# Packing the token-mixing product of a spectral and MLP block to eleven matmuls, with the shift by tokens made in SBUF

## The chip, the core and the metric

The kernel runs on one core of a Trainium2 chip. A core has five engines that run side by side, each with its own queue of instructions, worked off in order: TensorE (matmuls, "PE" in the profile; "PEld" is its loading of the stationary operand), VectorE ("DVE"), ScalarE ("ACT"), GpSimd ("POOL") and SyncE ("SP"), which here issues all DMA transfers. Sixteen DMA engines move the data. Engines wait for one another by semaphores. Matmuls write to PSUM (banks of 128 x 512 float32), the other tiles live in SBUF (128 partitions).

The metric is the device time of one execution in microseconds, as the median of several runs.

## The reference

x has 2048 tokens of 448 channels. It is normalized once (`xn`), and then two branches are added to it: a spectral filter (2-D FFT, product with a complex weight, inverse FFT) and an MLP block with a shift between tokens.

```python
def _A_ref(x, w_r, w_i):
    X = rfft2(x) * (w_r + 1j * w_i)
    return irfft2(X, s=(S, D))

def _B_ref(x, w1, w2, w3, w4):
    h = _gelu(_layernorm(x) @ w1)              # D x D
    c = D // 4                                 # 112 channels
    # four groups of channels, shifted by +1, -1, +2, -2 tokens, zeros come in
    hs = concatenate([g0, g1, g2, g3]) @ w2    # D x D
    x1 = x + hs
    return x1 + _gelu(_layernorm(x1) @ w3) @ w4   # 448 -> 1792 -> 448

xn = _layernorm(x)
out = x + _A_ref(xn, w_r, w_i) + _B_ref(xn, w1, w2, w3, w4)
```

The change touches the first half of `_B_ref`: the product with w1, the gelu, the shift and the product with w2.

## The kernel before

**Tiles.** Token 16a + b lies on partition a of block b: 16 blocks of 128 tokens. A shift by one or two tokens therefore mostly means another block on the same partition; only where the block number wraps (from 15 to 0 or from 0 to 15) the partition moves by one. Blocks are worked in four groups of four, `GRP = [[14, 15, 0, 1], [2, 3, 4, 5], [6, 7, 8, 9], [10, 11, 12, 13]]`. `load_x` loads two blocks at a time.

**Precision.** All large products are made of float16 halves: an operand is split in a high part and a low part (`hi`, `lo`), and a product takes the passes hi x hi, hi x lo and lo x hi (`PASS`), summed in PSUM. ScalarE makes the high part, VectorE (or GpSimd) the low part as a difference. Weights are scaled by a power of two first; `powers` finds it from a sum of squares (`squares`, on ScalarE), a small matmul with a tile of ones and a few steps on VectorE.

**The first half of the MLP block, in stages.**
- `norm1(g, apply)` normalizes a group: statistics on VectorE, then the blocks by the engines in `apply`; `refine` and `scales`, on GpSimd, make a finer scale (`gsc`) and the factor `cs` used later.
- `T1(g)` transposes a group on TensorE (16 transposes) and splits the result into `xT` (`transpose_split`: the high part on ScalarE, the low part on VectorE). The last group goes through `turn`, with DMA transposes.
- `w1_in` multiplies: 11 products of 448 columns for each block, four blocks in a group. For the first group all four blocks go along together, one quarter `t` of the channels after another.
- `w1_unit(g, i)` finishes a block: gelu on ScalarE, high part on ScalarE, low part on VectorE, both into a staging buffer `hs` with each 112-channel group padded to 128; then SP issues one DMA transpose of 8 pieces of 128 x 128 into `h`.
- `w2_tile(b)` multiplies with w2. The shift is made here, by reading for each of the four channel groups another block of `h`, at an offset of one column where the partition moves: four groups, three passes, so 12 products with 112 rows each. VectorE adds the result to xb(b).
- `ln2` is the second layer norm, ending with a DMA transpose for each block into `x2all`; `mlp` runs w3, gelu and w4 for eight pairs of blocks G.

**Order.** Each engine's order is made by a scheduler, which places instructions by priorities and its own estimate of times when the program is built; `behind(...)` holds an instruction back until named others have been issued. After that the order is fixed, so an instruction that waits holds everything behind it on its engine. `warm_up` puts 28 products on zeros at the start of TensorE's queue.

The spectral branch (from `do_fold` on) and the rest of the MLP follow and are not changed but for names of blocks.

Of the kernel before, what the change touches and what calls it, by code (L numbers as in the profile page):

```python
# [25 lines left out]
SHIFT = [1, -1, 2, -2]  # L26
WARM = 28
# [9 lines left out]
HS = 3  # L37
# [31 lines left out]
def constants():  # L69
# [20 lines left out]
    for c in range(NC):  # L90
        for j8, (k1, t) in enumerate(slots(c)):
            for j, (kr, s, base) in enumerate(rows(c)):
                if base != k1:
                    continue
                phi = tau * np.outer(np.arange(NB), kr + 128 * np.arange(16)) / S
# [28 lines left out]
def body(tc, nc, x, wf, w1, w2, w3, w4, c_g, c_n, c_small, out):  # L124
# [81 lines left out]
    SY.dma_start(w2s[:112], w2.rearrange("(k p) n -> p k n", p=112))  # L206
# [14 lines left out]
    x2mem = pw.tile([128, 9 * F], F16, name="x2mem")  # L221
    x2all = x2mem[:, 0:8 * F].rearrange("p (j t n) -> p j t n", j=4, t=7)
    w4raw = x2mem.bitcast(F32)[:, F:].rearrange("p (f n) -> p f n", f=14)
    w4v = w4.rearrange("(f p) n -> p f n", p=128)
    W4F = (0, 4, 8, 11, 14)

    def load_w4(i):
        SY.dma_start(w4raw[:, W4F[i]:W4F[i + 1]], w4v[:, W4F[i]:W4F[i + 1]])
# [164 lines left out]
    w2p = pr.tile([112, 2, 4, D], F16, name="w2p")  # L393
# [3 lines left out]

    def h_alloc(g):
        t = {0: 0, 1: 1, 2: 2, 3: 1}[g]
        hT[g] = pr.tile([128, 8, 512 if g else 592], F16, tag=f"h{t}", name=f"h{g}")  # L400
        if g == 0:
            P.memset(hT[g][:, :, 0:576].rearrange("p t (b a) -> p t b a", b=4)[:, :, :, 0:16], 0.0)
            P.memset(hT[g][:, :, 576:592], 0.0)

    def h_at(g, i):
        return 128 * i if g else 144 * i + 16
# [9 lines left out]

    hs_buf = [p1.tile([128, 2, 4, 128], F16, name=f"hs{i}") for i in range(HS)]
    for t in hs_buf:
        P.memset(t.rearrange("p i k n -> p (i k) n")[:, :, 112:], 0.0)

    for o in (0, 1024):
        hs_buf.append(x2mem[:, o:o + 1024].rearrange("p (i k n) -> p i k n", i=2, k=4))
        P.memset(hs_buf[-1].rearrange("p i k n -> p (i k) n")[:, :, 112:], 0.0)

    def w1_unit(g, i, pm=None):
        if pm is None:
            pm = bank(("tr" if g == 1 else "mm", "acc")[i // 2], f"pw1_{g}{i}")
            w1_in(g, [(i, pm)], range(4))
        c = CS[GRP[g][i]]
        pm = pm[:, :D]  # L430
        pv_ = pm.rearrange("p (k n) -> p k n", k=4)
        h = hs_buf[c % (HS if g == 3 else HS + 2)]
        A.activation(out=pm, in_=pm, func=AF.Gelu_apprx_tanh, scale=gsc[:, c:c + 1])
        u = A.activation(out=h[:, 0, :, 0:112], in_=pv_, func=AF.Copy, scale=h1)
        v = V.scalar_tensor_tensor(out=h[:, 1, :, 0:112], in0=pv_, scalar=h1, in1=h[:, 0, :, 0:112],
                                   op0=ALU.mult, op1=ALU.subtract)
        o = h_at(g, i)
        d = SY.dma_start_transpose(out=hT[g][:, :, o:o + 128], in_=h.rearrange("p i k n -> p (i k n)"))
        after[g, i] = u.ins, v.ins
        after["h", g, i] = (d.ins,)  # L440

    def w2_tile(b):
        pm = bank("sp", f"pw2_{b}")
        n = 0
        for k in (2, 0, 1, 3):
            src, o = b - SHIFT[k], 1
            if src < 0:
                src, o = src + NB, 0
            elif src >= NB:
                src, o = src - NB, 2  # L450
            g, i = WHERE[src]
            o += h_at(g, i) - 1
            for hi, wi in ((0, 0), (0, 1), (1, 0)):
                T.matmul(pm[:, :D], hT[g][:112, 4 * hi + k, o:o + 128], w2p[:, wi, k], start=n == 0, stop=n == 11)  # L454
                n += 1
        V.scalar_tensor_tensor(out=xb(b), in0=xb(b), scalar=cs[:, CS[b]:CS[b] + 1], in1=pm[:, :D],
                               op0=ALU.mult, op1=ALU.add)

    def ln2(bs, engines):
# [22 lines left out]
        for i in range(n):  # L482
            b, h, x_ = b0 + i, y[i // 2][:, i % 2], o[i // 2][:, i % 2]
            k = r[:, i:i + 1]
            u = A.activation(out=h[:, 0:D], in_=x_, func=AF.Copy, scale=k)
            V.scalar_tensor_tensor(out=h[:, 448:512], in0=x_[:, 384:448], scalar=k, in1=h[:, 384:448],
                                   op0=ALU.mult, op1=ALU.subtract)
            v = V.scalar_tensor_tensor(out=h[:, 512:896], in0=x_[:, 0:384], scalar=k, in1=h[:, 0:384],
                                       op0=ALU.mult, op1=ALU.subtract)
            d = SY.dma_start_transpose(out=x2all[:, b // 4][:, :, 128 * (b % 4):128 * (b % 4) + 128], in_=h)  # L490
            after[f"b{b0}"] = u.ins, v.ins, d.ins

    def unscale(p, part):
        t = part.rearrange("p (b n) -> p b n", b=2)
        SY.dma_start(t, xv[:, 2 * p:2 * p + 2])
        return lambda: V.scalar_tensor_tensor(out=xt[p], in0=xt[p], scalar=p12, in1=t, op0=ALU.mult, op1=ALU.add)

    def finish(b):
        t = xb(b)
        if b < 2:  # L500
            t = row()[:, :D]
            SY.dma_start(t, xv[:, b])
            V.scalar_tensor_tensor(out=t, in0=xb(b), scalar=p12, in1=t, op0=ALU.mult, op1=ALU.add)
        SY.dma_start(ov[:, b], t)
# [6 lines left out]
    def do_fold(b0):  # L511
        X = pfd.tile([128, 2, D + 1], F32, tag="xf", bufs=3, name=f"xf{b0}")
        after["X", b0] = (SY.dma_start(X[:, :, 0:D], xv[:, b0:b0 + 2]).ins,)
# [181 lines left out]
    def front(G, fp, tag):  # L695
        tok = slice(256 * (G % 2), 256 * (G % 2) + 256)
        pm = bank(tag, f"pw3_{G}{fp}")
        for ff in range(2):
            f = 2 * fp + ff
            mlp_in(pm[:, 256 * ff:256 * ff + 256], w3p, slice(128 * f, 128 * f + 128), x2all[:, G // 2], tok)  # L700
# [66 lines left out]
    def back(G, fp):  # L767
# [10 lines left out]
        for i in range(2):  # L778
# [12 lines left out]
            if end:  # L791
                with prio(EVAC):
                    for r, to in parts:
                        V.scalar_tensor_tensor(out=xb(b)[:, r], in0=to, scalar=p34[:, min(G, 1):min(G, 1) + 1],  # L794
                                               in1=xb(b)[:, r], op0=ALU.mult, op1=ALU.add)
                        if G > 4:
                            SY.dma_start(ov[:, b, r], xb(b)[:, r])
# [51 lines left out]
    def w4_split(f):  # L849
        split_w(w4p[0][:, 0, f:f + 2], w4p[0][:, 1, f:f + 2], w4raw[:, f:f + 2], s4)  # L850
# [7 lines left out]
    h_alloc(0)  # L858
# [8 lines left out]
    for t in range(4):  # L867
        w1_in(0, list(enumerate(first)), [t])
    n1[0][0]()
    with behind("w1", 1):  # L870
        n1.append(norm1(1, [P, V, A, V]))
    with behind("w1", 3):
        squares(m2[:112], flat(w2s[:112]))
# [20 lines left out]
    h_alloc(1)  # L894
# [10 lines left out]
    h_alloc(2)  # L905
# [17 lines left out]
    for b in range(4, 8):  # L923
        w2_tile(b)
        with behind(*PIN[b - 4]):
            w3_split(2 * b - 8)
            w3_split(2 * b - 7)
            for i in (2 * b - 10, 2 * b - 9):
                if i >= 0:
                    squares(m4[:, i:i + 1], flat(w4raw[:, 2 * i:2 * i + 2]), junk4)  # L930
    squares(m4[:, 6:7], flat(w4raw[:, 12:14]), junk4)
    ln2([2, 3], [A, P])
    h_alloc(3)
# [11 lines left out]
    for j in range(4):  # L945
        homes[j] = x2mem[:, F * j:F * j + F]
# [122 lines left out]
```

## Time and profile before

| | |
|---|---|
| median of 3 runs | 410.78 us (410.74 to 410.94) |
| profiled execution: time, span | 410.65 us, 408.9 us |
| TensorE busy | 402.3 us, 98% of the span, 3409 matmuls |
| VectorE busy | 330.7 us, 81% |
| ScalarE busy | 256.5 us, 63% |
| GpSimd busy | 95.3 us, 23% |
| products with w1 (L414) / with w2 (L454) | 176 / 192 |
| DMA transposes of h | 16, landing 3.2 to 3.5 us after issue |

Busy time of TensorE counts a matmul from its start to its modelled end, and matmuls overlap; the spacing of matmuls in the chain of work is the better measure of what one costs. The timeline's rows are: start, duration, engine, line, operation, output and inputs, shape, and how many of them were merged; in square brackets the idle time before it and what ended it. The rows of a table by windows give for each stretch TensorE, weight loads, VectorE, ScalarE and GpSimd as busy us with the number of instructions, then the granted clock, the DMA share and GB/s.

### The profile page before, as it was taken

Reading aid. Unit: us, or ns where it says so; the run is one execution under the profiler, and the core shown is the slowest. Engines: PE = TensorE matmul, PEld = TensorE weight load, DVE = VectorE, ACT = ScalarE, POOL = GpSimd, SP = SyncE. Lnnn points to the kernel's source line nnn. Section 1 sums busy time; section 2 is a strip of 40 time slices with the busy share of each in tenths; the row PEclk is TensorE's granted clock in tenths of the full one; section 3 lists DMA queues with packets and bytes.
Section 4 is the critical chain, followed back from the end, with each engine's and each line's share of the span. In section 5 each row is a group of like instructions: output and inputs, shape, how many; then the busy total and the mean of one; then the engine's idle time right before and its main releaser. Section 6 shows DMA issues by size and latency. Waiting matters only on the chain.

```text
span 408.9 us, 8745 instructions
## 1 busy us (share of the span) xinstructions
PE 402.3 (98%) x3409; PEld 299.0 (73%) x3409; DVE 330.7 (81%) x686; ACT 256.5 (63%) x434; POOL 95.3 (23%) x172
## 2 busy tenths in 40 slices
PE   7999999999999999999999999999999999999996
PEld 3655555765668777777887887877777779998995
DVE  4888999898857678887798888955899989966645
ACT  4698879973758866556598888863453554453431
POOL 3877720101336748400012111110000000000000
PEclk9999999999999999999999999999999999999999
DMA  8959879914786456516255666500011022100101
GB/s 278 354 192 179 153 149 321 177 62 90 156 231 202 137 196 210 170 59 183 63 145 143 155 156 171 147 27 3 24 68 69 25 88 85 55 2 2 45 2 45
DMA packets 56168, 51.28 MB, mean 125 GB/s; under 512 B 37632, under 2 KB 50496, under 8 KB 56128
## 3 DMA queue, kind: packets, MB, share of 16 engines
q1 hardware_dynamic: 56128, 50.74, 46.0%
q8 instruction: 26, 0.43, 0.4%
q14 instruction: 14, 0.11, 0.1%
HBM read 38.28 MB, written 3.67 MB: 103 GB/s over the span
## 4 chain that ended last, share of the span: by engine, by line
PE 94%; DVE 3%; DMA 2%; POOL 0%; issue 0%; ACT 0%; SPq 0%; POOLq 0%
PE pw L385 33%; PE acc L787 23%; PE pw L454 9%; PE pw L414 6%; PE side L757 4%; PE acc L757 3%; PE pu L646 3%; PE ps L543 3%; PE pe L667 2%; PE pp L601 2%; PE px L618 2%; PE py L688 2%; DVE sta L293 1%; DMA xt<-x 1%; DMA h<-hs 1%; PE pta L374 1%
## 5 line engine op out<-in xcount | busy, mean ns | idle before, releaser
L385 PE MATMUL pw<-x2mem,w3p 128*128 128x256 f16 x1232 | 151.1, 273 | 0.0
L385 PEld LDWEIGHTS <-w3p 128*128 128x128 f16 x1232 | 119.2, 98 | 20.6
L787 PE MATMUL acc<-w4p,hf 128*128 128x448 f16 (+1 forms) x516 | 105.4, 348 | 0.0
L787 PEld LDWEIGHTS <-hf 128*128 128x128 f16 x516 | 49.8, 98 | 36.5
L705 ACT ACTIVATE pw<-pw,pe 128x512 f32<-128x512 f32 x42 | 27.5, 655 | 35.7 <-PE pw L385 35.7
L708 DVE SCALAR_TENSOR_TENSOR hf<-pw,h,hf 128x512 f16<-128x512 f32 x42 | 31.3, 748 | 14.5 <-ACT hf L707 14.4
L454 PE MATMUL pw<-w2p,h 112*128 112x448 f16 x192 | 39.9, 352 | 0.8 <-DMA h<-hs 0.8
L414 PE MATMUL pw<-w1p,xT 128*128 128x448 f16 x176 | 35.4, 352 | 0.0
L627 POOL TENSOR_TENSOR z<-te 128x450 f32<-128x450 f32 x16 | 15.7, 982 | 70.3 <-DVE te L625 70.3
L454 PEld LDWEIGHTS <-h 112*128 112x128 f16 x192 | 18.6, 98 | 17.2 <-DMA h<-hs 1.0
L707 ACT ACTIVATE hf<-pw,h 128x512 f16<-128x512 f32 x42 | 28.7, 686 | 1.0
L414 PEld LDWEIGHTS <-xT 128*128 128x128 f16 x176 | 16.9, 98 | 16.4 <-DVE xT L379 0.8
L723 ACT ACTIVATE hz<-g,h 128x896 f16<-128x896 f32 x14 | 14.6, 1044 | 22.3 <-DVE g L720 22.2
L757 PEld LDWEIGHTS <-hz 128*128 128x128 f16 x294 | 28.2, 98 | 0.4
L608 ACT ACTIVATE pf<-pp 64x450 f16<-64x450 f32 x32 | 17.4, 544 | 12.3 <-DVE pf L609 8.0
L609 DVE TENSOR_TENSOR pf<-pp,pf 64x450 f16<-64x450 f32 x32 | 19.9, 622 | 3.4 <-ACT pf L608 3.0
L724 DVE SCALAR_TENSOR_TENSOR hz<-g,h,hz 128x896 f16<-128x896 f32 x14 | 16.1, 1150 | 7.6 <-ACT hz L723 7.6
L623 ACT ACTIVATE te<-px 64x450 f32<-64x450 f32 x32 | 17.3, 542 | 1.2 <-PE px L618 0.6
L526 POOL TENSOR_TENSOR f<-xr 128x452 f32<-128x452 f32 x16 | 16.4, 1046 | 0.6
L717 ACT ACTIVATE g<-pw,pe 128x512 f32<-128x512 f32 x14 | 9.6, 684 | 10.2 <-PE pw L385 10.1
L794 DVE SCALAR_TENSOR_TENSOR xt<-acc,p,xt 128x448 f32<-128x448 f32 (+1 forms) x17 | 10.9, 654 | 6.2 <-PE acc L787 6.0
L523 POOL TENSOR_TENSOR xr<-xf 128x452 f32<-128x452 f32 x8 | 9.7, 1211 | 26.7 <-issue 20.3
(183 smaller groups left out, 705.7 us busy)
## 6 DMA issues: line engine op xcount, KB each, us to landing
wc<-wf SPq DMA_DIRECT2D x32, 225.0 KB, 3.8
wl<-wf SPq DMA_DIRECT2D x8, 450.0 KB, 4.1
xt<-x SPq DMA_DIRECT2D x8, 448.0 KB, 7.9
xf<-x SPq DMA_DIRECT2D x8, 448.0 KB, 3.6
loads<-x SPq DMA_DIRECT2D x7, 448.0 KB, 4.0
out<-xt SPq DMA_DIRECT2D x13, 224.0 KB, 1.9
w3raw<-w SPq DMA_DIRECT2D x3, 896.0 KB, 12.6
gn<-c_g SPq DMA_DIRECT2D x16, 128.0 KB, 3.1
```

The costliest lines, as they stand in the source:

```text
L385: T.matmul(ps_out, wp[:, wi + t, cols], xT[:, xi + t, tok], start=t == 0 and wi + xi == 0, stop=t == 3 and wi == 4)
L414: T.matmul(pm[:, :D], xTs[g][:, xi + t, 128 * i:128 * i + 128], w1p[:, wi + t], start=t == 0 and p == 0, stop=t == 3 and p == 2)
L454: T.matmul(pm[:, :D], hT[g][:112, 4 * hi + k, o:o + 128], w2p[:, wi, k], start=n == 0, stop=n == 11)
L526: P.tensor_tensor(out=f[:, :, k:k + 2].rearrange("p b s d -> p s b d"), in0=u[:, :, 0], in1=u[:, :, 1], op=op)
L608: A.activation(out=hi, in_=src, func=AF.Copy)
L609: V.tensor_tensor(out=lo, in0=src, in1=hi, op=ALU.subtract)
L623: A.activation(out=e[64 * h:64 * h + 64], in_=px_[64 - 64 * h:128 - 64 * h, :2 * DF], func=AF.Copy)
L705: A.activation(out=pm, in_=pm, func=AF.Gelu_apprx_tanh, scale=r3)
L707: i = A.activation(out=h[:, 0], in_=pm, func=AF.Copy, scale=h3)
L708: j = V.scalar_tensor_tensor(out=h[:, 1], in0=pm, scalar=h3, in1=h[:, 0], op0=ALU.mult, op1=ALU.subtract)
L757: m = T.matmul(to, h[:, hi, 128 * blk:128 * blk + 128], b[wi], start=new and n == 0, stop=n == 2 and (last if blk in (2, 5, 3, 0) else end ...
L787: m = T.matmul(to, h[:, hi, o:o + 128], w4p[0][:, wi, f, r], start=first and f % 2 == 0 and n == 0, stop=end and f % 2 == 1 and n == 2, sk ...
```

## The change

- **Packing.** The channels of h are put in the order of `TURN` (w1's columns and w2's rows are permuted on the host). `w1_unit` no longer writes a block's h into one staging buffer, but each 112-channel group into the `slot` of the block that needs it after the shift (`slots_of`, four slots at once). The low part on VectorE becomes two instructions of 224 columns. Four scratch groups wrap around; `wrap` copies them by DMA from SBUF to SBUF with the partition moved by one, 127 partitions. A slot holds 448 high and 448 low channels without padding, 7 pieces of 128, and is transposed by DMA when all that goes into it is there (`DONE` names which blocks are complete after which unit).
- **Eleven products.** `w2_tile` takes 3 pieces of high parts with w2's high and low parts (6 products), one mixed piece (the last 64 high channels and first 64 low ones) with a weight tile of its own, and 4 products of the pieces with low parts with w2's high part: 11, on 128 rows. w2 is split on 128 partitions, and two DMA copies of 64 rows place shifted copies of its halves.
- **First group.** The first group's products go together for two quarters, then block by block. `refine` of the first group is held behind the split of w1's last quarter. Units 0 and 1 are finished ahead of the rest.
- **Loads.** x is loaded in the order of `GRP`, with blocks renamed by two (`at_token`), so the first two blocks used come first. w2 comes in two transfers. w4 is loaded partly into a tile of its own, since `x2mem` now holds the slots.
- Warm-up products go from 28 to 24, and the scratch memory for software DMA is made smaller.

```diff
-SHIFT = [1, -1, 2, -2]
-WARM = 28
+TURN = [3, 1, 0, 2]
+DONE = {c: [c - 2] for c in range(2, 12)} | {12: [10, 13], 13: [11, 12, 14, 15]}
+FIRST = 2
+WARM = 24
...
+    def at_token(b):
+        return (b + FIRST) % NB
...
     def load_x(g):
-        for b0 in sorted(GRP[g])[::2]:
-            SY.dma_start(xt[b0 // 2], xv[:, b0:b0 + 2])
+        for b0 in GRP[g][::2]:
+            SY.dma_start(xt[b0 // 2], xv[:, at_token(b0):at_token(b0) + 2])
...
-    SY.dma_start(w2s[:112], w2.rearrange("(k p) n -> p k n", p=112))
+    P.memset(w2s[64:128, 3], 0.0)
+    SY.dma_start(w2s[:, 0:3], w2[0:384].rearrange("(t p) n -> p t n", p=128))
+    SY.dma_start(w2s[0:64, 3], w2[384:448])
...
-    x2mem = pw.tile([128, 9 * F], F16, name="x2mem")
+    x2mem = pw.tile([128, 10 * F], F16, name="x2mem")
+    w4half = [x2mem.bitcast(F32)[:, 2 * F:2 * F + 4 * D].rearrange("p (f n) -> p f n", f=4),
+              p1.tile([128, 10, D], F32, name="w4half")]
...
-    w2p = pr.tile([112, 2, 4, D], F16, name="w2p")
+    w2p = pr.tile([128, 11, D], F16, name="w2p")
+    P.memset(w2p[64:128, 10], 0.0)
...
+    def slot(b):
+        return x2mem[:, 896 * b + 3584:896 * b + 4480].rearrange("p (i n) -> p i n", i=2)
+
+    def slots_of(c, i):
+        t = slot(c - 2)[:, i]
+        return bass.AP(t.tensor, t.offset, [list(t.ap[0]), [3 * 896 + 224, 2], [896 + 112, 2], [1, 112]])
+
+    def wrap(to, own, by, k):
+        dst, src = slot(to)[:, :, k], slot(own)[:, :, k]
+        SY.dma_start(dst[1:128] if by else dst[0:127], src[0:127] if by else src[1:128])
+
+    for b, by, k in ((-2, 1, slice(224, 448)), (-1, 1, slice(336, 448)), (12, 0, slice(0, 112)), (13, 0, slice(0, 224))):
+        P.memset(slot(b)[0:1, :, k] if by else slot(b)[96:128, :, k], 0.0)
...
     def w1_unit(g, i, pm=None):
...
-        u = A.activation(out=h[:, 0, :, 0:112], in_=pv_, func=AF.Copy, scale=h1)
-        v = V.scalar_tensor_tensor(out=h[:, 1, :, 0:112], in0=pv_, scalar=h1, in1=h[:, 0, :, 0:112],
-                                   op0=ALU.mult, op1=ALU.subtract)
-        o = h_at(g, i)
-        d = SY.dma_start_transpose(out=hT[g][:, :, o:o + 128], in_=h.rearrange("p i k n -> p (i k n)"))
+        u = A.activation(out=h[0], in_=pv_, func=AF.Copy, scale=h1)
+        for k in range(2):
+            v = V.scalar_tensor_tensor(out=h[1][:, k], in0=pv_[:, k], scalar=h1, in1=h[0][:, k],
+                                       op0=ALU.mult, op1=ALU.subtract)
         after[g, i] = u.ins, v.ins
+        if GRP[g][i] == 13:
+            wrap(-2, 14, 1, slice(224, 448))
+            wrap(-1, 15, 1, slice(336, 448))
+        for b in DONE.get(GRP[g][i], ()):
+            if b // 4 not in hT:
+                hT[b // 4] = pr.tile([128, 7, 512], F16, tag="h", bufs=2, name=f"h{b // 4}")
+            d = SY.dma_start_transpose(out=hT[b // 4][:, :, 128 * (b % 4):128 * (b % 4) + 128],
+                                       in_=slot(b if b < 14 else b - 16).rearrange("p i n -> p (i n)"))
...
     def w2_tile(b):
         pm = bank("sp", f"pw2_{b}")
-        n = 0
-        for k in (2, 0, 1, 3):
...
-            for hi, wi in ((0, 0), (0, 1), (1, 0)):
-                T.matmul(pm[:, :D], hT[g][:112, 4 * hi + k, o:o + 128], w2p[:, wi, k], start=n == 0, stop=n == 11)
-                n += 1
+        h = hT[b // 4][:, :, 128 * (b % 4):128 * (b % 4) + 128]
+        for n, (k, w) in enumerate([(k, w) for k in range(3) for w in (k, k + 7)] + [(3, 10)] + [(k, k) for k in (3, 4, 5, 6)]):
+            T.matmul(pm[:, :D], h[:, k], w2p[:, w], start=n == 0, stop=n == 10)
...
-    for t in range(4):
+    for t in range(2):
         w1_in(0, list(enumerate(first)), [t])
-    n1[0][0]()
+    for unit in enumerate(first):
+        w1_in(0, [unit], [2, 3])
+    with behind("w1", 3):
+        n1[0][0]()
...
+    for k in range(2):
+        w1_unit(0, k, first[k])
     with behind("a1"):
-        w1_unit(0, 0, first[0])
         n1.append(norm1(2, [P, V, A, P]))
     with behind("a1"), behind("n", 2):
-        for k in range(1, 4):
+        for k in range(2, 4):
             w1_unit(0, k, first[k])
+    wrap(12, -4, 0, slice(0, 112))
+    wrap(13, -3, 0, slice(0, 224))
     with behind("na", 2):
         for k in range(4):
-            split_w(w2p[:, 0, k], w2p[:, 1, k], w2s[:112, k], s2[:112], P)
+            r = slice(0, 128 if k < 3 else 64)
+            split_w(w2p[r, k], w2p[r, 7 + k], w2s[r, k], s2[r], P)
+        SY.dma_start(w2p[64:128, 3:7], w2p[0:64, 0:4])
+        SY.dma_start(w2p[0:64, 4:7], w2p[64:128, 0:3])
...
-    nc = bacc.Bacc("TRN2", target_bir_lowering=False, num_devices=1)
+    nc = bacc.Bacc("TRN2", target_bir_lowering=False, num_devices=1, dynamic_dma_scratch_size=1024)
```

In the order that results, SP issues the first two `wrap` copies just ahead of the first transpose of h, and the last two behind the transposes for blocks 8, 9, 10 and 13 and ahead of two transposes of `ln2` and of those for blocks 11, 12, 14 and 15. On TensorE the product of block b with w2 follows as one piece of 11, where before it was cut in pieces of three as blocks of h arrived.

More of the change, by code (lines that the diff above doesn't have):

```diff
@@ L430, in w1_unit @@
         pm = pm[:, :D]
-        pv_ = pm.rearrange("p (k n) -> p k n", k=4)
-        h = hs_buf[c % (HS if g == 3 else HS + 2)]
+        pv_ = pm.rearrange("p (i j n) -> p i j n", i=2, j=2)
+        h = [slots_of((GRP[g][i] + 2) % NB - 2, k) for k in range(2)]
         A.activation(out=pm, in_=pm, func=AF.Gelu_apprx_tanh, scale=gsc[:, c:c + 1])
-        u = A.activation(out=h[:, 0, :, 0:112], in_=pv_, func=AF.Copy, scale=h1)
-        v = V.scalar_tensor_tensor(out=h[:, 1, :, 0:112], in0=pv_, scalar=h1, in1=h[:, 0, :, 0:112],
-                                   op0=ALU.mult, op1=ALU.subtract)
@@ new lines, in w1_unit @@
+        if GRP[g][i] == 13:
[6 more added lines that the diff above has]
+                                       in_=slot(b if b < 14 else b - 16).rearrange("p i n -> p (i n)"))
+            after["h", g, i] = (d.ins,)
@@ L945, in body @@
     for j in range(4):
-        homes[j] = x2mem[:, F * j:F * j + F]
+        homes[j] = x2mem[:, F * (j ^ 2):F * (j ^ 2) + F]
     w4t.update({j: m.rearrange("p (i k n) -> p i k n", i=2, k=4) for j, m in homes.items()})
```

63 lines of the change are left out of this document (19 added, 44 removed).

## The prediction

> **What bounds the kernel now.** I read the page's busy times and slices first, then TensorE's waits, then the chain in order of time.
>
> ```profile
> span 408.9 us, 8745 instructions
> PE 402.3 (98%) x3409; PEld 299.0 (73%) x3409; DVE 330.7 (81%) x686; ACT 256.5 (63%) x434; POOL 95.3 (23%) x172
> PE   7999999999999999999999999999999999999996
> ...
> PE wps L817 <- DVE wsrc L187: 1.2, 1, 1.2
> PE pm L249 <- DVE pt L247: 1.1, 1, 1.1
> PE pw L454 <- DMA h<-hs: 0.8, 1, 0.8
> ...
> 10.28 1.94 PE pta L374 x16
> 12.23 8.41 PE pw L414 x44
> 96.43 2.27 PE pw L454 x12
> 106.47 2.29 PE pw L385 x21
> ```
>
> TensorE stands still only for the three waits of 1.2, 1.1 and 0.8 us and in the last slice: every matmul removed counts in full, and every new wait of TensorE adds in full, because its queue is in order. The chain gives the spacing: 1.94/16 = 0.12 us for a transpose, 8.41/44 = 0.191 for a first-layer product, 2.27/12 = 0.189 for a token-mixing product, 2.29/21 = 0.109 for a w3 product.
>
> **Products removed.** Sixteen blocks go from 12 products to 11; a product costs the same with 112 or 128 rows: 16 x 0.189 = 3.0 us less, all on the path. Nothing else on TensorE is smaller but four warm-up products (below).
>
> **The opening.** These rows are the timeline of before.
>
> ```profile
> 1.22 7.53 PE L817 MATMUL wps<-wsrc 128*128 128x512 f16 x28 [1.22 <-DVE wsrc L187]
> 8.43 0.58 ACT L242 ACTIVATE xr<-w1s 64x448 f16<-64x448 f32 x1
> 9.00 0.75 ACT L320 ACTIVATE xt<-xt,nma,vy 128x448 f32<-128x448 f32 x1
> 9.90 0.38 PE L249 MATMUL pm<-pt,ones 128*128 128x1 f32 x2 [1.15 <-DVE pt L247]
> 10.32 0.16 DVE L251 TENSOR_SCALAR pt<-pm 128x1 f32<-128x1 f32 x1 [0.47 <-PE pm L249]
> 16.09 1.39 DVE L379 TENSOR_TENSOR xT<-pta,xT 128x512 f16<-128x512 f32 x2
> 18.69 0.20 POOL L332 TENSOR_TENSOR vq<-vy 128x8 f32<-128x8 f32 x1 [0.59 <-DVE vy L313]
> 19.03 1.18 POOL L323 TENSOR_SCALAR xt<-xt,vy,nma 128x448 f32<-128x448 f32 x1
> 20.48 1.47 PE L374 MATMUL pta<-ident,xt 128*128 128x128 f32 x12
> 21.12 2.05 ACT L378 ACTIVATE xT<-pta 128x512 f16<-128x512 f32 x4 [1.51 <-PE pta L374]
> 22.56 0.30 POOL L341 TENSOR_SCALAR gsc<-vr,pe 128x4 f32<-128x4 f32 x1
> 23.07 2.14 ACT L433 ACTIVATE pw<-pw,gsc 128x448 f32<-128x448 f32 x4
> 25.14 1.67 ACT L434 ACTIVATE hs<-pw,h 128x448 f16<-128x448 f32 x3
> 28.20 4.77 SPq L438 DMA_TRANSPOSE h<-hs  x3
> 30.81 1.27 DVE L435 SCALAR_TENSOR_TENSOR x2mem<-pw,h,x2mem 128x448 f16<-128x448 f32 x2
> 31.16 1.04 PE L374 MATMUL pta<-ident,xt 128*128 128x128 f32 x8
> 34.42 2.05 PE L454 MATMUL pw<-w2p,h 112*128 112x448 f16 x10
> ```
>
> x in order of use lets the statistics begin on the first tile while the second is in flight. But ScalarE now normalizes its x block (0.75) ahead of the fourth square of w1; that square, which the power of two for w1 needs, ends near 9.8 in place of 9.1, and the scalar product starts near 10.0 in place of 9.90. Gain zero, loss 0.1. Twenty-four warm-up products end about 0.85 earlier, so TensorE rests 2.1 us there in place of 1.15.
>
> First-layer products start near 12.25. Twenty-four end at 16.8; the unit-by-unit order then needs the low part of the fourth transposed piece at once, and VectorE has it at 17.5 (16.09 + 1.39; before, it was needed near 19). So 0.7 us of wait, and all 44 products end near 21.2 in place of 20.6. GpSimd, which no longer refines first, is through with w1's halves near 16.2; the refinement takes 3.0 (18.69 to 22.86 for group 1, less the 1.18 between), so its scale is there near 19.3 while the first gelu waits for ScalarE until 19.6, and the normalized block of group 1 (1.18, after two small steps) near 21.0, 0.6 ahead of its transposes: cost zero, and with that cover gone, what GpSimd is late by. The new memsets run while GpSimd waits.
>
> In the new order ScalarE handles units 0 and 1 ahead of and between group 1's splits. Unit 0's gelu waits for the scalar product of w2 (21.2) and VectorE's reading of it (0.42 later, as 9.90 to 10.32): gelu to 22.4, one split (0.5), copy to 23.6; its low half, now two instructions, is done at 24.7. Group 1's splits move back with it: VectorE has the last low part near 26.8 (24.7 and three of 0.7), 35 products of group 1 follow to 33.5, and group 2's 16 transposes end at 35.5.
>
> **The copies between slots.** This decides. The shift by tokens is now made in SBUF, and where it wraps, four copies of 127 partitions (two runs each, of 224 or 448 bytes) go through SP's queue: two when units 0 and 1 are done, ahead of the first transpose; two after the last unit, ahead of two transposes for the second layer norm and of three of the last four transposes of h. No copy of before has such a shape (all have 128, 112 or 64 rows). The prices come from three transposes and from the output stores at the end:
>
> ```profile
> DMA  0000000000289999999994000000799999999964
> DMA packets 2140, 0.53 MB, mean 111 GB/s; under 512 B 2140, under 2 KB 2140, under 8 KB 2140
> q1 hardware_dynamic: 2140, 0.53, 59.5%
> h<-hs SPq DMA_TRANSPOSE x3, 3.2
> ...
> DMA packets 432, 0.46 MB, mean 27 GB/s; under 512 B 48, under 2 KB 432, under 8 KB 432
> q1 hardware_dynamic: 432, 0.46, 7.7%
> ```
>
> The first window is 28.2 to 33 us: 0.595 x 16 engines x 4.8 us over 2140 packets is 21 ns for 256 bytes. The second is 392 to 409: 0.077 x 16 x 17 over 432 is 48 ns, or 53 for its 384 rows of 1.2 KB. So 20 ns for 224 bytes, 28 for 448, and a pair of copies, 254 runs each, holds 254 x (20 + 28) = 12.2 us of engine time. The 48 small packets of three stores are 16 for each: a copy goes in equal shares to 16 engines, each closing with one packet. 127 rows have no equal shares between 2 and 16 engines. Either all go through one engine (12.2 us, and all later transfers, which need that engine too, wait behind), or unequal shares over 16 (0.8 us). No row shows which; I take one engine, because every copy of the trace is in equal shares.
>
> [...]
>
> First pair: issued at 24.8; first packet 1.2 later (the first busy slice of the first window above); 12.2 on the engine; then the first transpose, 2.0 from first packet to landing (3.2 - 1.2): 40.2. TensorE has come to that transpose's product at 35.5 and stands 4.7 us. In before, the same point (group 2 transposed, two token products done) is 34.42, with 408.9 - 34.4 = 374.5 us still to go; after 40.2 fourteen of the removed products lie ahead, so 374.5 - 14 x 0.189 = 371.9. The halves of w2 moved to other partitions (two copies of 64 rows behind that transpose) are needed 12 products, 2.3 us, later: hidden.
>
> Second pair:
>
> ```profile
> 64.87 4.33 PE L414 MATMUL pw<-w1p,xT 128*128 128x448 f16 x22
> 73.74 6.62 SPq L438 DMA_TRANSPOSE h<-hs  x4
> 80.00:85.00 5.00, 5.00 (x39) 3.63 (x38) 5.00 (x14) 4.51 (x8) 0.00 (x0) 1.00 0.75 187
> L435 DVE SCALAR_TENSOR_TENSOR hs<-pw,h,hs 128x448 f16<-128x448 f32 x12 | 7.9, 675 | 2.3 <-ACT hs L434 2.3
> L765 DVE SCALAR_TENSOR_TENSOR xt<-side,p,xt 128x224 f32<-128x224 f32 x3 | 1.3, 446 | 0.0
> ```
>
> In before the last transpose of h is issued at 73.74 + 3/4 x 6.62 = 78.7, 9.5 us after the last first-layer product (69.2); about 1.3 of that was the wait for a staging buffer that is gone. I take 8 us (bounds 1.9, one gelu, copy and low half, and 9.5). Block 11's token product stands 80 w3 products and three blocks behind that product: 80 x 0.109 + 33 x 0.189 = 15.0. Its transpose lands 8 + 1.2 + 12.2 + 2 x 1.2 (the layer norm's transposes) + 2.0 = 25.8 after it. Wait: 10.8 us. Blocks 12, 14 and 15 follow at 1.2 each, faster than the products use them.
>
> **Restart of the clock.** The windows of the warm-up:
>
> ```profile
> 1.20:2.20 1.00, 0.98 (x3) 0.43 (x4) 1.00 0.60 82
> 4.20:5.20 1.00, 1.00 (x7) 0.45 (x5) 1.00 1.05 393
> ```
>
> TensorE begins at about half rate (3 products in the first us against 7 in the fourth), which costs 7.53 - 28 x 0.216 = 1.5 us (0.216 is 0.189 x 512/448); after the rest of 1.15 us there is none of it. For each new rest the bounds are 0 and 1.5: I take 1.5 for 10.8 us and 0 for 4.7 and 2.1.
>
> [...]
>
> **Sum.** 40.2 + 371.9 + 10.8 + 1.5 = 424.4 of span; around the span lie 410.65 - 408.9 = 1.75 in the profiled execution, whose time is 0.13 under the median of the runs. Forecast 426 us. VectorE's 16 low halves, two instructions each (2 x 446 - 675 = 217 ns more, 3.5 us together), cost nothing here: TensorE waits longer.
>
> **Rivals.** (1) Unequal shares over 16 engines; the change does what it says. The first transpose is then issued when VectorE has the low halves of units 0 to 3 and of group 1's first (30.81 + 1.27 = 32.1 in before; near 33.0 with about 1 us of longer halves ahead) and lands at 36.2; the second wait vanishes (8 + 1.2 + 0.8 + 2.4 + 2.0 = 14.4, under 15.0). 36.2 + 371.9 + 1.75 = 409.8; with the opening at before's pace down to 407.7, faster. It decides when the second pair is off the engine within 1.4 us. For: the bytes are few. Against: equal shares. (2) The same, but VectorE, full in this stretch (5.00 of 5.00 at 80 to 85), passes its extra instructions on: 12 of the 16 lie there, 12 x 0.217 = 2.6, so 412.4. For: that row. Against: TensorE had no wait there at all. (3) One engine, but small runs that go singly cost nearer 34 ns (midway between 21 and 48): 17.2 a pair, 5.0 more at each, 436.
>
> **Numbers.** One engine 0.85 (with the third rival, 0.15 of it), the first rival 0.09, the second 0.06. The likeliest case alone runs from 416 (21 ns a run, so 10.9 a pair, copies issued 1.9 after the last product, no restart) to 436. The range takes in the first rival: 410 to 436. What a measurement here can tell is 0.2%, 410.0 to 411.6: faster 0.07, same 0.04, slower 0.89.
>
> **What would show it.** Right: TensorE waits for the transpose of h twice, 3 to 6 us near 35 and 5 to 12 near 89; the landing of the 127-row copies is 5 to 9 us each though they are tiny; DMA share near 0.06 while they run; fewer products per us after the second wait. Token products fall from 192 to 176, spacing 0.189. Wrong: the copies land in about 2 us and TensorE's waits for h sum to under 2 us.

## The result, and the profile after

The changed kernel takes 420.89 us (median of four runs, 420.24 to 422.28); the kernel before, on the same chip, 410.81. The ratio is 1.025, 95% interval 1.0223 to 1.0276: slower by 10.1 us, where 15 were forecast (426, range 410 to 436). The profiled execution took 420.24 us, its span is 418.5, 9.6 more than before.

The page of the changed kernel begins with:

```profile
span 418.5 us, 8724 instructions
...
PE 401.9 (96%) x3389; PEld 297.6 (71%) x3389; DVE 333.0 (80%) x702; ACT 255.9 (61%) x434; POOL 95.4 (23%) x171
```

TensorE's waits (us in total, times, longest):

```profile
PE pw L463 <- DMA h<-x2mem: 9.3, 3, 6.6
PE pm L260 <- DVE pt L258: 1.7, 1, 1.7
...
PE pw L416 <- DVE xT L390: 0.6, 2, 0.3
PE pw L416 <- DMA xT<-x: 0.2, 1, 0.2
```

The token-mixing products among the groups (busy us, mean ns | idle before):

```profile
L463 PE MATMUL pw<-w2p,h 128*128 128x448 f16 x176 | 37.2, 367 | 9.3 <-DMA h<-x2mem 9.3
```

TensorE is as busy as before (402.3 then) and simply stands still for longer. TensorE's timeline (start, us, what, [idle before and its releaser]) shows where:

```profile
10.28 0.38 PE L260 MATMUL pm<-pt,ones 128*128 128x1 f32 x2 [1.68 <-DVE pt L258]
...
23.24 1.14 PE L416 MATMUL pw<-w1p,xT 128*128 128x448 f16 x3 [0.32 <-DVE xT L390]
24.67 8.11 PE L416 MATMUL pw<-w1p,xT 128*128 128x448 f16 x41 [0.30 <-DVE xT L390]
...
35.99 1.31 PE L463 MATMUL pw<-w2p,h 128*128 128x448 f16 x6 [1.46 <-DMA h<-x2mem]
...
74.77 2.25 PE L463 MATMUL pw<-w2p,h 128*128 128x448 f16 x11 [1.27 <-DMA h<-x2mem]
...
79.26 4.33 PE L463 MATMUL pw<-w2p,h 128*128 128x448 f16 x22
...
93.16 6.46 PE L463 MATMUL pw<-w2p,h 128*128 128x448 f16 x22 [6.60 <-DMA h<-x2mem]
```

And SP's queue, in the same columns:

```profile
23.74 3.45 SPq L430 DMA_DIRECT2D x2mem<-x2mem  x2
...
78.47 5.08 SPq L430 DMA_DIRECT2D x2mem<-x2mem  x2
83.65 6.28 SPq L498 DMA_TRANSPOSE x2mem<-y  x2
89.98 6.26 SPq L455 DMA_TRANSPOSE h<-x2mem  x4
```

The rests of 1.46 and 6.60 us each follow a pair of copies; the one of 1.27 us, at block 8, does not. The 22 products behind the longest take 6.46 us, where the 22 at 79.26 take 4.33. Windows of the stretch (each engine's busy us, then the granted clock, the DMA share, GB/s) tell why for both:

```profile
28.00:30.00 2.00, 2.00 (x13) 1.00 (x11) 1.86 (x13) 1.75 (x4) 0.98 (x5) 1.00 0.07 16
82.00:84.00 2.00, 2.00 (x15) 1.21 (x14) 1.77 (x8) 2.00 (x4) 0.00 (x0) 1.00 0.07 21
90.00:92.00 2.00, 0.00 (x0) 0.00 (x0) 0.00 (x0) 0.21 (x1) 0.13 (x1) 0.67 0.98 185
92.00:94.00 2.00, 0.84 (x3) 0.40 (x4) 0.95 (x4) 2.00 (x4) 0.51 (x1) 0.50 0.84 159
```

While copies run, the sixteen DMA engines together are 0.07 busy, about one of sixteen, at 16 to 21 GB/s. In the last part of the long rest the granted clock is 0.67, and behind it 0.50.

The 9.6 us of span add up from these rows: h's waits 9.3 - 0.8 = +8.5, the first scale product 10.28 - 9.90 = +0.4, xT's waits +0.8, another 0.6 inside the three products at 23.24 (1.14 for what takes 3 x 0.19 = 0.57 by the usual spacing), the throttled clock 6.46 - 4.33 = +2.1, sixteen products -3.0. That is 9.4.

### The profile page after: what moved, and what is told of

Same layout as the page of the kernel before. It is cut to its first block, busy times and chain, and to the rows that moved or that the text cites. A ratio compares the mean times of both kernels' runs of the same rounds, so it can differ in the third digit from the quotient of the medians.

```text
span 418.5 us, 8724 instructions
## 1 busy us (share of the span) xinstructions
PE 401.9 (96%) x3389; PEld 297.6 (71%) x3389; DVE 333.0 (80%) x702; ACT 255.9 (61%) x434; POOL 95.4 (23%) x171
## 4 chain that ended last, share of the span: by engine, by line
PE 81%; DMA 6%; DVE 5%; ACT 4%; SPq 2%; POOL 1%; issue 1%; ACTq 0%; POOLq 0%
PE pw L396 30%; PE acc L795 23%; PE side L765 4%; PE pw L416 3%; PE pw L463 3%; PE acc L765 3%; PE pu L654 3%; PE ps L551 3%; PE pe L675 2%; PE pp L609 2%; DMA h<-x2mem 2%; PE px L626 2%; PE py L696 2%; DMA x2mem<-w 2%; ACT xr L253 2%; SPq L498 1%
## 5 line engine op out<-in xcount | busy, mean ns | idle before, releaser
L463 PE MATMUL pw<-w2p,h 128*128 128x448 f16 x176 | 37.2, 367 | 9.3 <-DMA h<-x2mem 9.3
L463 PEld LDWEIGHTS <-h 128*128 128x128 f16 x176 | 17.5, 101 | 26.8 <-DMA h<-x2mem 10.4
L542 DVE TENSOR_TENSOR xh<-f,xh 128x452 f16<-128x452 f32 x16 | 13.0, 846 | 6.6 <-ACT xh L541 6.6
L534 POOL TENSOR_TENSOR f<-xr 128x452 f32<-128x452 f32 x16 | 17.5, 1115 | 0.6
L484 ACT ACTIVATE y<-xt,nm 128x448 f32<-128x448 f32 x8 | 5.4, 669 | 18.3 <-DMA x2mem<-y 13.7
L725 ACT ACTIVATE g<-pw,pe 128x512 f32<-128x512 f32 x14 | 9.5, 682 | 10.2 <-PE pw L396 10.1
```

The costliest lines, as they stand in the source:

```text
L463: T.matmul(pm[:, :D], h[:, k], w2p[:, w], start=n == 0, stop=n == 10)
L534: P.tensor_tensor(out=f[:, :, k:k + 2].rearrange("p b s d -> p s b d"), in0=u[:, :, 0], in1=u[:, :, 1], op=op)
```

## The experiments

Theory A: a copy of 127 rows runs on one DMA engine, and the transfers behind it wait. Theory B: SP's issue of these copies is what costs, whatever the engines. Theory C: other parts of the change cost.

**One row across the cut.** Two versions differ in one number, `n`: 112 or 113.

```diff
-        SY.dma_start(dst[1:128] if by else dst[0:127], src[0:127] if by else src[1:128])
+        for a, b in ((0, n), (n, 127)):
+            SY.dma_start(dst[a + by:b + by], src[a + 1 - by:b + 1 - by])
```

> Each shift copy of 127 rows is issued as two, of 112 and of 15 rows; nothing else is edited (the planner moves a few of the third layer's matmuls). [...] Theory B (what costs is the issue of a partition-shifted copy on SP's queue, 3.45 and 5.08 us for two): four issues a pair instead of two, so at least 420.9 and up to 429. Theory C (VectorE's halves, the opening or w4's loads make the time): 420.9 as before.

> As the split into 112 and 15 rows, but cut one row later: 113 and 14 rows. The same number of transfers and bytes, the same order on every engine. Theory A: 113 is prime, so 226 runs of the pair's 254 stay on one engine for each copy: a pair takes about 8 us instead of 9, the longer rest falls from 6.6 to 5 to 6 us, the first from 1.46 to 0.5: 418.5 to 420.5. If the engine count isn't what costs (a shift of partitions, short runs, the second transfer, the issue), the time is that of 112 and 15 rows within 0.5 us.

Measured: 416.71 us with 112 and 15 rows (414.95 to 418.16; ratio 1.0141, 1.0116 to 1.0165), 421.13 with 113 and 14 (420.76 to 421.69; 1.0248, 1.0232 to 1.0263). One window of 112 and 15 rows (the profiled run is the fastest of five), and its rests for h on the timeline:

```profile
28.00:30.00 2.00, 2.00 (x13) 1.00 (x11) 1.87 (x12) 1.74 (x4) 0.98 (x6) 1.00 0.01 2
```

```profile
74.46 2.25 PE L464 MATMUL pw<-w2p,h 128*128 128x448 f16 x11 [1.30 <-DMA h<-x2mem]
...
89.43 4.33 PE L464 MATMUL pw<-w2p,h 128*128 128x448 f16 x22 [1.87 <-DMA h<-x2mem]
```

The same window and the rests of 113 and 14 rows:

```profile
28.00:30.00 2.00, 2.00 (x12) 1.07 (x11) 1.90 (x11) 1.70 (x3) 1.07 (x6) 1.00 0.06 13
```

```profile
35.60 1.31 PE L464 MATMUL pw<-w2p,h 128*128 128x448 f16 x6 [0.75 <-DMA h<-x2mem]
...
93.91 6.69 PE L464 MATMUL pw<-w2p,h 128*128 128x448 f16 x22 [5.73 <-DMA h<-x2mem]
```

One row more in the first piece, with the same number of transfers, bytes and the same order on every engine, costs 4.4 us. With 112 rows the engines are idle at 28 us (0.01 busy) because the copies are over (the four of the first pair land 2.1 to 3.5 us after issue); with 113 they are still at about one of sixteen (0.06). B expected the same time for both and falls. A holds, and the rest with 113 rows (5.73 against 6.60) is shorter about as 226 runs are fewer than 254. But the split version isn't at 420.9 - 1.5 - 6.6 - 2.1 = 410.7, where it would be if A were all and both rests and the throttled clock went: 6 us are left, 4 in the execution profiled. Of these 4, 1.7 are two waits of TensorE for VectorE in the spectral branch, at 139 and 163 us, that the changed kernel doesn't have.

**No copies.**

```diff
-    wrap(12, -4, 0, slice(0, 112))
-    wrap(13, -3, 0, slice(0, 224))
-            wrap(-2, 14, 1, slice(224, 448))
-            wrap(-1, 15, 1, slice(336, 448))
-        P.memset(slot(b)[0:1, :, k] if by else slot(b)[96:128, :, k], 0.0)
+        P.memset(slot(b)[:, :, k], 0.0)
```

> No shift copies at all: the parts of the four end blocks that they fill are set to zero once, so the tokens whose taps reach across a 128-row edge of the sequence's ends get zeros there, and that part of the product is left out. All matmuls run. Theory A: this is the floor of the split, 409.5 to 411. Theory C (other parts of the change cost): 415 to 421, with the same rests.

This kernel leaves out the copies and puts zeros where they would write. Measured: 414.20 us (413.49 to 414.73; ratio 1.0077, 1.0063 to 1.0091). Taken by itself this says that the copies cost 420.9 - 414.2 = 6.7 us and that the rest of the change, which should have won 1, loses 3.2. TensorE's waits there:

```profile
PE pw L460 <- DMA h<-x2mem: 3.3, 5, 1.4
PE pm L260 <- DVE pt L258: 1.9, 1, 1.9
...
PE pw L416 <- DVE xT L390: 0.6, 2, 0.3
```

A window of its opening:

```profile
12.00:14.00 2.00, 2.00 (x9) 1.13 (x8) 2.00 (x5) 2.00 (x6) 0.39 (x1) 0.50 1.06 310
```

The waits for h are spread (five, the longest 1.4, at block 8), group 1's products wait for their low parts, and in this execution the clock fell to 0.50 behind the opening's rest of 1.9 us. So C is right too, for 3.2 us at most: the scheduler made an order of its own for this version, with the load of the spectral constants ahead of the last five transposes of h, and a rest of 1.18 us at block 9 that the other versions don't have.

**The copies moved, whole and split.** The first pair goes behind the transposes of blocks 0 to 3, the second behind those of blocks 11 and 12.

```diff
-    wrap(12, -4, 0, slice(0, 112))
-    wrap(13, -3, 0, slice(0, 224))
...
     for k in range(4):
         w1_unit(1, k)
+    with behind("h", 1, 3):
+        wrap(12, -4, 0, slice(0, 112))
+        wrap(13, -3, 0, slice(0, 224))
...
-        if GRP[g][i] == 13:
-            wrap(-2, 14, 1, slice(224, 448))
-            wrap(-1, 15, 1, slice(336, 448))
         for b in DONE.get(GRP[g][i], ()):
+            if b == 14:
+                with behind("h", g, i):
+                    wrap(-2, 14, 1, slice(224, 448))
+                    wrap(-1, 15, 1, slice(336, 448))
```

> The copies keep their 127 rows but are issued later: the first pair behind the transposes of blocks 0 to 3 (blocks 12 and 13 are the first to need it), the second pair behind the transposes of blocks 11 and 12 (only 14 and 15 need it). Theory A with the place in SP's queue deciding: a pair still takes about 9 us on one engine, the first rest of 1.46 us is gone, blocks 10 to 13 can be multiplied while the second pair runs (44 products, 8.6 us, and what is left of the first third-layer group), so the rest of 6.6 us shrinks to 0 to 3 us at blocks 14 and 15, and the clock stays up: 409.5 to 414. If the length of the copies costs wherever they stand (the transfers of y behind them become the new wait): 417 to 421.

> The copies split into 112 and 15 rows and issued late: the first pair behind the transposes of blocks 0 to 3, the second behind those of blocks 11 and 12. Theory (place matters once the length is mended): the rest of 1.87 us at block 11 goes, as in the version without copies, and nothing else waits: 414.0 to 415.5, within a microsecond of the 414.2 without copies. Rival (the second pair, a little later, holds up blocks 14 and 15 by as much): 416 to 417.5.

Measured with 127 rows: 419.44 us (417.89 to 419.72; ratio 1.0198, 1.0182 to 1.0213), in the range where the length costs wherever it stands. TensorE's timeline in that version:

```profile
56.18 3.68 PE L464 MATMUL pw<-w2p,h 128*128 128x448 f16 x11 [3.21 <-DMA h<-x2mem]
...
99.74 3.94 PE L464 MATMUL pw<-w2p,h 128*128 128x448 f16 x11 [2.03 <-DMA h<-x2mem]
```

SP's queue:

```profile
39.95 3.41 SPq L430 DMA_DIRECT2D x2mem<-x2mem  x2
43.41 5.34 SPq L222 DMA_DIRECT2D w3raw<-w  x2
48.85 1.25 SPq L456 DMA_TRANSPOSE h<-x2mem  x1
```

The rests moved to block 4 and to block 14, and the clock fell behind each (3.68 and 3.94 us for 11 products instead of 2.25). SP's own issues are held as well: the two loads of w3 take 5.34 us behind the copies, 1.22 in the changed kernel, where transposes stand ahead of them, and 1.73 behind the copies once they are split. The median of this version also holds a loss that comes ahead of the copies: in its profile the clock fell in the opening too, where 44 products take 9.63 us instead of 8.59.

Measured with 112 and 15 rows: 412.11 us (411.77 to 413.96; ratio 1.0028, 1.0016 to 1.004). Length and place together make up 420.9 - 412.1 = 8.8 of the 10.1 us; length alone 4.2, place alone 1.5 (by the medians; place alone would have won more without the fall of the clock in the opening). It is also 2 us faster than the version without copies, so that one wasn't the floor; what the rest of the change loses is nearer 1 us than 3.

**The warm-up back to 28** (on the split version).

```diff
-WARM = 24
+WARM = 28
```

> The copies split into 112 and 15 rows, and the 28 warm-up matmuls of before in place of 24; no other instruction moves. In the profiles with 24 the rest ahead of the first scale product is 1.68 to 1.94 us against 1.15 before, and in two of five profiles (copies moved, no copies) the granted clock falls to 0.50 behind it, 16 transposes and 44 products taking 2.5 and 9.6 us instead of 1.95 and 8.6. Theory: the shorter warm-up costs through that rest: the rest comes down to about 0.9, the clock stays at 1.0 in all runs, and the median of the split version falls from 416.7 by 0.3 to 1.5 us with less spread: 415.2 to 416.4. Rival: the throttled clock of those profiles has nothing to do with the warm-up: 416.7 with the same spread.

Measured: 417.28 us (414.64 to 418.25; ratio 1.0135, 1.0108 to 1.0162), no change that can be told from 416.71. The rest ahead of the first scale product is gone from the waits, yet four of the six runs have a mean granted clock of 0.994 to 0.996 and take 417.2 to 418.3, and two at 0.999 or 1.0 take 414.6 and 414.8. The theory fell for this version: the clock goes with the spread of its times, but the opening's rest can't be all of it. Where the clock falls in the four longer runs isn't shown, since the profile is of a run with the full clock; the rests that remain there are 1.62 us at block 8 and 2.06 at block 11. In the split and moved version, which hasn't the second, seven of nine runs have the full clock. Its profile is of one of the other two (413.44 us), and there the fall is in the opening (the changed kernel takes 8.59 us for these products):

```profile
9.88 0.38 PE L260 MATMUL pm<-pt,ones 128*128 128x1 f32 x2 [1.81 <-DVE pt L258]
...
12.65 9.41 PE L416 MATMUL pw<-w1p,xT 128*128 128x448 f16 x44
```

The two best versions below, moved as well and with 28 warm-up products, have the full clock in all 23 runs. So once the copies are moved the longer warm-up may pay after all; two of nine against none of 23 is too little to show it.

**The opening put back** (on the split version): the first group's products all end together, its units and scales come as before.

```diff
-    for t in range(2):
+    for t in range(4):
         w1_in(0, list(enumerate(first)), [t])
-    for unit in enumerate(first):
-        w1_in(0, [unit], [2, 3])
-    with behind("w1", 3):
-        n1[0][0]()
+    n1[0][0]()
...
-    for k in range(2):
-        w1_unit(0, k, first[k])
     with behind("a1"):
+        w1_unit(0, 0, first[0])
         n1.append(norm1(2, [P, V, A, P]))
     with behind("a1"), behind("n", 2):
-        for k in range(2, 4):
+        for k in range(1, 4):
```

> The copies split into 112 and 15 rows, and the opening put back: the first group's 44 products all end together as before, its scales and first unit come where they came before. Theory (the new opening costs): the wait ahead of group 1's products (0.62 us shown and 0.57 us inside the first three) goes, 415 to 416. Rival (the new opening pays, since unit 0's gelu and halves start 1 to 2 us earlier): 417 to 419, with a rest ahead of the second layer's first product.

Measured: 414.93 us (413.57 to 418.09; ratio 1.0106, 1.0075 to 1.0136). The intervals of the two openings overlap, so this stays open; in the runs with the full clock it is 413.6 to 414.4 against 415.0 to 416.7. Its profile has no wait for xT, and a new one of 2.05 us at the second layer's start (37.77 us); block 8 rests 2.47 us for 1.30 and block 11 no longer rests. The two openings trade one wait for another.

**w4's loads.** First three of the four loads at about 40 us (on the split version):

```diff
     with behind("h", 1, 3):
         load_w3([3])
+        for i in (1, 2, 3):
+            load_w4(i)
```

> The copies split into 112 and 15 rows, and w4's second to fourth load (2.3 MB) issued behind the transposes of blocks 0 to 3, some 22 us earlier; only the first load stays in its place. Theory: the rest of 1.30 us ahead of block 8 (in every version of the changed kernel between 0.4 and 1.4) is the transposes of block 8 queued behind w4's loads, so it goes: 415.0 to 415.8. Rivals: the block waits for its VectorE half, whatever the loads do: 416.7; or the early loads hold up the transposes of blocks 4 to 7 instead: 417 to 419.

Measured: 416.37 us (415.29 to 419.2; ratio 1.0136, 1.011 to 1.0161). The rest at block 8 is gone and another of 2.34 us stands at block 4, whose transpose now needs 9.1 us from issue to landing behind the early loads, in place of 3. Then ScalarE's order instead (on the split and moved version, with 28 warm-up products):

```diff
-            for i in (2 * b - 10, 2 * b - 9):
-                if i >= 0:
+            for i in (2, 3, 4, 0, 1, 5)[2 * max(b, 5) - 10:2 * b - 8]:
+                if b > 4:
```

> The version with the copies split and moved (412.1), with two small edits: 28 warm-up matmuls, and ScalarE's squares of w4 take the parts in w4half first and those in x2mem later. In the split and moved version ScalarE stands 2.71 us at 73.4 for the load of w4 into x2mem, with unit 10's half behind it in its queue, and block 8 rests 1.81 us. Theory (the rest at block 8 is ScalarE's order, not the DMA queue's): the rest falls to 0 to 0.6 us; and with 28 warm-up matmuls the clock stays up in the opening in every run: 409.8 to 411.0, at or just under the kernel before. Rival (block 8's transposes are held by w4's loads themselves): the rest stays at 1.3 to 1.8 us and the time at 411.5 to 412.

Measured: 411.22 us (410.51 to 412.04; ratio 1.0007, 0.9998 to 1.0016): the time of the kernel before. The halves behind the squares moved from 74.4 to 70.2 us, and block 8 still rests 1.52: this theory fell. The halves that moved are those of units 11 and 12. Block 8 is complete with unit 10 (`DONE`), whose high half is done at 57.3 us, ahead of the splits of w3, so this edit couldn't reach it. Its transpose is issued at 64.13 us, behind w4's loads, and lands 10.1 us later, where the others mostly need 3.1. That points at the queue. So last, two of the loads at 46 us, behind block 4's transposes:

```diff
+    with behind("h", 2, 0):
+        load_w4(2)
+        load_w4(3)
```

> The version with split and moved copies, 28 warm-up matmuls and the new order of the squares (411.2), and two of w4's four loads (1.38 MB of 3.2, into a buffer of their own) issued behind block 4's transposes at about 46 us instead of at 62. Moving ScalarE's squares brought unit 10's next halves 4 us forward and left block 8's rest at 1.52 us, so what holds it is the queue: w4's loads took 5.9 to 9.2 us from issue to landing there, and block 8's transposes stand behind them. Theory: with half the loads gone from that place block 8's transposes land by 68, the rest of 1.52 goes, the loads fit where the DMA rows are a half busy, and xT, 8 us ahead of its use, isn't held: 409.2 to 410.4, faster than the kernel before. Rival (the loads at 46 hold up xT and block 5 as the earlier load of 2.3 MB held up block 4): a rest of 1 to 2 us at 56 to 59 in place of the one at 74, 411 to 414.

Measured: 411.25 us (410.48 to 411.87; ratio 0.9998, 0.999 to 1.0007). From its timeline:

```profile
57.08 2.25 PE L465 MATMUL pw<-w2p,h 128*128 128x448 f16 x11 [0.86 <-DMA h<-x2mem]
...
71.19 2.24 PE L465 MATMUL pw<-w2p,h 128*128 128x448 f16 x11
```

From its waits:

```profile
PE pw L416 <- DMA xT<-x: 0.7, 2, 0.3
...
PE ps L553 <- DVE y L558: 0.6, 1, 0.6
PE acc L797 <- ACT hf L717: 0.4, 1, 0.4
```

Block 8 (at 71.19) no longer waits, which confirms that w4's loads held it (in the version of 416.37 its rest went with them too); the waits came back smaller at block 5 and elsewhere. No version here beats the kernel before by what can be measured.

**VectorE's halves behind the splits** (on the version of 411.22), unit 1's alone and then unit 0's too:

```diff
-    for k in range(2):
-        w1_unit(0, k, first[k])
+    w1_unit(0, 0, first[0])
     with behind("a1"):
+        w1_unit(0, 1, first[1])
```

> As the version with 28 warm-up matmuls and the new order of the squares, with unit 1's halves behind group 1's splits on VectorE instead of ahead of them (the planner then also puts the whole first part of the third layer ahead of blocks 8 and 9). Theory: the wait of TensorE for the low halves of group 1 (0.62 us shown, 0.57 inside the first three products) loses one VectorE instruction pair of 0.80 us ahead of it, 0.5 to 1 us off: 409 to 410.5. Rival (the later halves hold up the first transposes of h, and the other plan costs): 411 to 414.

> As the last, with unit 0's halves behind the splits too. Theory: the wait of group 1's products goes altogether, 1.2 us off against the version with the new order of the squares: 408.8 to 410. Rival (the first h transposes come later and TensorE rests ahead of the second layer): 411 to 414.

Measured: 419.88 us (ratio 1.0224, 1.0208 to 1.0239) and 420.57 (1.0232, 1.0218 to 1.0246). The waits for the low parts did shrink (0.16 and 0.17 us in the first), but the scheduler made another order of everything after. ScalarE and TensorE of the first of the two:

```profile
60.89 7.55 ACT L279 ACTIVATE w3p<-w3raw,pe 128x896 f16<-128x896 f32 x8
68.35 0.61 ACT L445 ACTIVATE x2mem<-pw,h 128x448 f16<-128x448 f32 x1
...
76.50 3.98 PE L465 MATMUL pw<-w2p,h 128*128 128x448 f16 x11 [5.38 <-DVE y L498]
```

Unit 10's half now stands behind the eight splits of w3 on ScalarE (before, ahead of them, at 56.6 us), so block 8's transpose is late and TensorE rests 5.38 us, with the clock down after it (3.98 us for 11 products instead of 2.25). What the halves cost by themselves isn't answered by these two.

## Why the prediction was right, and where it was off

**Right in its deciding step.** "I take one engine" was the choice between two readings that no row could settle; the pair of 112 and 113 rows settles it. While the copies of 127 and 113 rows run, the sixteen engines are 0.07 and 0.06 busy, about one of them; the copy of 112 rows with runs of 448 bytes brings them to 0.8 and 0.9 in two slices of 0.15 us from 27.05 us on, and all copies of that pair are over by 28 us. That it comes of shares that can't be equal, as the prediction argues, is the author's reading and not shown by these runs. Both forecast waits are there, at 36 and at 93 us, and behind the longer one the granted clock is 0.50. The second has the forecast size (6.60 us, 5 to 12 forecast), the first has not (1.46, 3 to 6 forecast).

**The price of a run: off.** "254 x (20 + 28) = 12.2 us" for a pair. The DMA view of the changed kernel between 25.6 and 28.6 us, where the copy with runs of 224 bytes is under way, and between 29.6 and 32.6, where the one with 448 is (packets, MB, share):

```profile
q1 hardware_dynamic: 232, 0.05, 7.7%
...
q1 hardware_dynamic: 142, 0.06, 7.4%
```

That is 3.0 us for 232 packets and 3.0 for 142: 12.9 and 21.1 ns each, so 254 x (12.9 + 21.1) = 8.6 us for a pair. The rows quoted for the price were transposes and output stores, with the sixteen engines 0.9 busy or more in their fullest slices; a copy inside SBUF on one engine is cheaper than both. Whether that comes of the SBUF or of the engine being alone, no run tells. This takes 3.6 us off each wait: the whole difference of the first (1.46 for 4.7) and most of the second's (6.60 for 10.8), and it is the largest part of what made 426 too long.

**The time of issue: off by 1.** "Unit 0's gelu waits for the scalar product of w2 (21.2)" is wrong: it doesn't wait. These rows are ScalarE and VectorE of the changed kernel.

```profile
19.76 0.59 ACT L443 ACTIVATE pw<-pw,gsc 128x448 f32<-128x448 f32 x1
...
21.22 0.80 DVE L446 SCALAR_TENSOR_TENSOR x2mem<-pw,h,x2mem 128x224 f16<-128x224 f32 x2
```

The gelu runs at 19.76, the low half is done at 22.0 and not 24.7, and SP begins with the copies at 23.74 for 24.8. TensorE comes to the first product that waits about 1 us earlier too (34.5 for 35.5), so the first wait gains nothing by it. The second pair is issued 8.5 us after the last first-layer product (78.47 against 70.0), 8 were taken. TensorE comes to the product that waits at 86.5, 16.5 us behind that product and not 15.0, which shortened the second wait by as much; 1.3 of it is the rest at block 8, which lies in between.

**The clock: right in kind.** 1.5 us for the longer rest, measured 2.1; none for the shorter, measured none. The step that set the bounds at 0 and 1.5 was too narrow.

**"VectorE's 16 low halves ... cost nothing here", and the opening: wrong.** For copies that don't hold anything up the forecast's own sum was the first rival's, 409.8. The nearest versions measured 412.1 (split and moved) and 414.2 (none). What was put down as hidden comes out as waits: 0.6 us for xT and 0.6 inside the first three products of group 1, because units 0 and 1 put their halves (0.80 us each) ahead of group 1's splits on VectorE; and 1.27 us at block 8, which the prediction doesn't have at all. There the changed order puts a transpose of h into SP's queue just behind w4's loads, where before (73.74 us) it came when they were through. "So 0.7 us of wait" isn't there: group 0's 44 products run without a stop. That group 1's wait has about this size is chance: it comes of the halves ahead of its splits, a delay that the prediction has as well (last low part near 26.8, measured 25.9) and that its wait for the copies would have covered.

**So two errors partly cancelled.** The one-engine copies were priced at 426 - 409.8 = 16 us and measured 8.8 (by the version that both splits and moves them), everything else was put at -1.0 and measured about +1.3. That 426 was only 5 us too long owes something to luck. The side and the cause were right, the sum of its parts was not.

**The other rivals.** The second (412.4, VectorE passes its extra instructions on) came nearer than the first to what is left when the copies hold nothing up, 412.1, but by luck: its place was wrong, since the wait it shows is in the opening and not at 80 us. The third (34 ns a run) is refuted by 12.9 and 21.1. The gain of sixteen products is real, 192 x 0.19 to 176 x 0.19, but in the best version, at 411.2, 2.8 us of small new waits (h 1.1 more, xT 1.1, 0.6 inside group 1's first products) take it back.

## What to carry to other kernels

Look at the row count of every copy before its bytes: tiny copies of 127 and of 113 rows (49 to 111 KB) kept about one of sixteen engines busy here (0.06 to 0.07) and held the transfers behind them in the queue, and one row more or fewer, 113 or 112, was worth 4.4 us, 1% of this kernel. Which other row counts do the same was not measured. When such a transfer is found, mend both its length and its place, and measure each by itself: here place alone won 1.5 us, length alone 4.2, both together 8.8. A saving on the busiest engine is worth only what the queues behind it leave: 3.0 us of products became 0 through waits of 0.2 to 1.5 us each.

## What was not expected

- **Rests of 1.7 to 2.5 us may or may not throttle TensorE.** In the profiles the clock fell behind rests of 1.70, 1.81, 1.94, 2.03, 2.13 and 2.34 us, and did not behind others of 1.68, 1.69, 1.74, 1.76, 1.81, 1.87, 2.05, 2.06 and 2.47; behind all four of 3.2 us and more (3.21, 5.38, 5.73 and 6.60) it fell. Each fall cost 1.4 to 2.4 us of slower products (11 in 3.68 us for 2.25, 22 in 6.69 for 4.33), so a kernel with such rests has two times, run by run (414.7 and 417.7 for the split one with 28 warm-up products). Of the eight profiles with 24 warm-up products, the clock fell in the opening in the three whose warm-up took the least time (6.85, 6.85 and 6.96 us) and in none of the five where it took 7.33 or more.
- **A one-engine copy also holds the queue that issues.** The two loads of w3 behind it took SP 5.34 us to issue instead of 1.22, and 1.73 behind the split ones.
- **A copy inside SBUF, on one engine, takes 12.9 ns for a run of 224 bytes and 21.1 for one of 448**, less than the 20 and 28 read from transposes and stores.
